# Turning the attention output of units 8 to 23 by DMA transposes instead of the PE, in a fused attention and MLP kernel

## Chip, cores, metric

One core of one Trainium2 chip. The metric is device time in microseconds (us) of one execution. One of 11 executions of the kernel before took 392 us in one series; it is not among the fast runs.

Names: PE is TensorE, which does the matmuls; ScalarE stands in profile lines as ACT, VectorE as DVE, GpSimd as POOL; SP is SyncE, which here issues the loads, the stores and the DMA transposes. PSUM is the memory that PE's products are written to.

## The reference

A linear attention with a decaying state feeds an MLP with SiLU. Cut to what matters:

```python
# r, k, v: (4 batches, 8 heads, 768 positions, 48)
for t in range(S):
    cur = einsum('bhd,bhe->bhde', u * kt, vt)
    y[:, :, t] = einsum('bhd,bhde->bhe', rt, state + cur)
    state = w[None, :, :, None] * state + einsum('bhd,bhe->bhde', kt, vt)
x = y.transpose(0, 2, 1, 3).reshape(3072, 384)
h = x @ w_in                      # 384 -> 2048
return (h * sigmoid(h)) @ w_out   # 2048 -> 384
```

## The kernel before

The sequence is cut into pieces of 128 positions. One piece of one batch is a **unit** (24 of them), and the four units of the same piece are a **chunk** `sc` (6 of them). The attention of a unit leaves `y16` with positions on the partitions. The first MLP product needs the 384 features on the partitions, so `p4` turns the tile: three PE transposes into PSUM and a ScalarE copy to `xT`.

```python
def p3e(i):
    L["y16"] = wrk.tile([128, H, D], F16, name="y16")
    nc.vector.tensor_tensor(out=L["y16"], in0=L["y"], in1=L["vu"], op=ALU.add)

def p4(i):
    ...                                    # xT: one tile for the four units of a chunk
    yT = ps.tile([128, NQ, C], F16, name="yT", tag="t", bufs=5)
    yf = L["y16"].rearrange("p h d -> p (h d)")
    for q in range(NQ):                    # NQ = 3
        nc.tensor.transpose(yT[:, q, :], yf[:, 128 * q:128 * q + 128], ident16)
    nc.scalar.copy(out=xts[sc][:, :, b, :], in_=yT)
```

The MLP of a finished chunk waits in a queue of **fillers**, which are put between the steps of the next units so that PE always has work: `l1` (three matmuls and a Silu on ScalarE; 512 columns wide, or 256 for half a chunk) and a quarter of an `l2` (four matmuls; after the fourth quarter DVE copies `osb` and SP stores it). `fill(n)` takes fillers worth n; a half-width `l1` counts one half.

```python
for i in range(B + 2, NU):                 # units 6 to 23
    ...                                    # p2: scores of unit i, then input transposes of i + 1
    fill(2)
    ...                                    # front: v cast on ScalarE, products on GpSimd for i + 1
    if i >= NIN:
        load(i + NIN)                      # r, k, v of unit i + 6: three DMAs on SP
    fill(1)
    p3y(i); p3e(i); sums(i); state(i)
    fill(2)
    p4(i)
    r16(i + 1)                             # cast of rT on ScalarE
    fill(1)
    ...
    fill(2)
    if b == B - 1:
        ...                                # l1 of the whole chunk, then its l2, join the queue
```

## Time and profile before

| | |
|---|---|
| median time | 201.92 us (201.52 to 202.05, 3 runs); 201.77 (4 runs) in the comparison with the changed kernel |
| span in the profile | 200.2 us |
| PE busy | 192.0 us, without a gap from 50 us to 197 us |
| transposes of `p4` | 72, three per unit; 0.168 us of PE per unit (units 8 to 23) |
| copies of `p4` on ScalarE | 24 x 0.478 us |
| loads, stores on SP | 72 of 192 KB, landing in 3.8 to 4.0 us; 23 of 192 KB, landing in 2.0 us |

PE's instructions overlap (three transposes of 220 ns each start within 0.17 us), so the busy length of one is not what it costs the next one. For the cost, read the time from the start of one group to the start of the next. The lines that carry this stand in the prediction.

### The profile page before, as it was taken

To read this page: it belongs to the slowest core of one execution; us is meant where nothing else is said; L and a number is where in the kernel's file an instruction comes from. 1 tells how busy PE (TensorE), PEld (TensorE's weight loads), DVE (VectorE), ACT (ScalarE), POOL (GpSimd) and SP (SyncE) were. 2 spreads that over 40 slices of the span, in tenths; PEclk is the share of its full clock that TensorE was granted. 3 is DMA by queue.
4 is the path that set the end of the run, shared out by engine and by line. 5 is a ranking of instruction groups with operands and counts; after the bars stand their busy time and mean duration, and the time that the engine had idled before them with its cause. 6 is when DMAs were issued, how large, how long until landed. Compare 5 with 4: busy or idle time off the path is not lost.

```text
span 200.2 us, 5013 instructions
## 1 busy us (share of the span) xinstructions
PE 192.0 (96%) x1973; PEld 129.8 (65%) x1973; DVE 115.1 (58%) x233; ACT 97.9 (49%) x225; POOL 115.2 (58%) x145
## 2 busy tenths in 40 slices
PE   7789999898999999999999999999999999999993
PEld 2546878786776976765666765666764666644563
DVE  6787658894757647773746864646863635510121
ACT  2655487798133652049662039662039661069300
POOL 3489969989865783768593767481748370100000
DMA  4999998999889954498521748201120001210022
GB/s 86 201 185 165 181 213 178 178 186 194 170 172 226 245 120 97 103 221 175 114 48 40 163 114 161 43 0 43 39 84 0 0 3 41 78 43 0 0 79 79
DMA packets 82207, 22.34 MB, mean 112 GB/s; under 512 B 75400, under 2 KB 82184, under 8 KB 82184
## 3 DMA queue, kind: packets, MB, share of 16 engines
q1 hardware_dynamic: 78504, 18.88, 43.7%
q0 software_dynamic: 3680, 3.15, 10.3%
q8 instruction: 15, 0.25, 0.5%
q14 instruction: 8, 0.07, 0.1%
HBM read 20.45 MB, written 4.72 MB: 126 GB/s over the span
## 4 chain that ended last, share of the span: by engine, by line
PE 84%; DVE 6%; POOL 4%; issue 3%; ACT 1%; DVEq 0%; POOLq 0%
PE ops L366 30%; PE hps L354 28%; PE ae L267 10%; PE xs L242 4%; PE y L293 3%; PE yT L342 2%; DVE am L276 2%; PE y L290 2%; POOL ku L180 1%; PE ops L380 1%; PE sps L309 1%; PE spin L125 1%; DVE pif L156 1%; POOL rku_f L186 1%; DVE y L300 1%
## 5 line engine op out<-in xcount | busy, mean ns | idle before, releaser
L357 ACT ACTIVATE gT<-hps 128x256 f16<-128x256 f32 (+1 forms) x128 | 59.5, 495 | 25.1 <-PE hps L354 23.3
L354 PE MATMUL hps<-xT,win 128*128 128x256 f16 (+1 forms) x384 | 69.9, 326 | 0.2
L366 PE MATMUL ops<-wout,gT 128*128 128x384 f16 x368 | 65.8, 326 | 0.0
L354 PEld LDWEIGHTS <-win 128*128 128x128 f16 x384 | 35.2, 98 | 22.1 <-issue 0.9
L366 PEld LDWEIGHTS <-gT 128*128 128x128 f16 x368 | 34.2, 98 | 20.9
L343 ACT COPY xT<-yT 128x384 f16<-128x384 f16 x24 | 11.5, 478 | 56.4 <-PE yT L342 56.4
L276 DVE TENSOR_TENSOR am<-ae,maskM 128x512 f16<-128x512 f32 x24 | 16.6, 691 | 32.5 <-PE ao L269 32.5
L203 POOL TENSOR_TENSOR vu<-vin,rku 128x384 f32<-128x384 f32 x23 | 19.1, 829 | 21.8 <-DVE rku L197 21.7
L370 DVE COPY osb<-ops 128x384 f32<-128x384 f32 x23 | 12.8, 556 | 32.5 <-PE ops L366 32.3
L267 PE MATMUL ae<-rk 48*128 48x128 f32 x192 | 27.7, 285 | 1.0 <-DVE rk L230 1.0
L267 PEld LDWEIGHTS ae<-rk 48*128 48x128 f32 x192 | 23.1, 187 | 8.3 <-issue 5.8
L269 PE MATMUL ao<-rk 48*128 48x128 f32 x192 | 27.7, 285 | 0.0
L253 DVE TENSOR_TENSOR rk<-xs,pif 112x512 f32<-112x512 f32 x40 | 25.6, 680 | 1.7 <-PE xs L242 1.7
L180 POOL TENSOR_TENSOR ku<-kin,u_bc 128x384 f32<-128x384 f32 x24 | 24.1, 1005 | 2.0 <-DMA kin<-in_k_dram 2.0
L186 POOL TENSOR_TENSOR rku_f<-rin,ku 128x384 f32<-128x384 f32 x24 | 24.1, 1005 | 1.9
L191 POOL TENSOR_TENSOR kc<-kin,lamC 128x384 f16<-128x384 f32 x24 | 24.0, 1002 | 0.0
L269 PEld LDWEIGHTS ao<-rk 48*128 48x128 f32 x192 | 23.1, 187 | 0.0
L323 POOL CAST stb<-st 112x384 f16<-112x384 f32 x12 | 6.0, 502 | 22.8 <-DVE st L318 22.8
L300 DVE TENSOR_TENSOR y<-y,vu 128x384 f16<-128x384 f32 x24 | 13.3, 554 | 8.7 <-PE y L293 6.5
L276 DVE TENSOR_TENSOR am<-ao,maskM 128x512 f16<-128x512 f32 x24 | 16.3, 680 | 0.0
L197 DVE TENSOR_REDUCE rku<-rku_f 128x8 f32<-128x384 f32 x24 | 13.2, 549 | 2.4 <-POOL rku_f L186 2.0
L325 POOL TENSOR_TENSOR sdec<-st,pif 112x384 f32<-112x384 f32 x16 | 13.3, 835 | 1.8 <-ACT gT L357 1.1
(74 smaller groups left out, 188.4 us busy)
## 6 DMA issues: line engine op xcount, KB each, us to landing
rin<-in_r_dram SPq DMA_DIRECT2D x24, 192.0 KB, 4.0
kin<-in_k_dram SPq DMA_DIRECT2D x24, 192.0 KB, 3.8
vin<-in_v_dram SPq DMA_DIRECT2D x24, 192.0 KB, 3.8
out_dram<-osb SPq DMA_DIRECT2D x23, 192.0 KB, 2.0
win<-in_moe_w_in_dram POOLq DMA_DIRECT2D x4, 384.0 KB, 6.0
wout<-in_moe_w_out_dram POOLq DMA_DIRECT2D x2, 768.0 KB, 10.4
out_dram<-osh SPq DMA_DIRECT2D x1, 128.0 KB, 1.7
out_dram<-osh SPq DMA_DIRECT2D x1, 64.0 KB, 1.5
```

The lines of the kernel that those rows point to most:

```text
L180: nc.gpsimd.tensor_tensor(out=L["ku"], in0=kin[i % NIN][:, :, 0:D], in1=u_bc, op=ALU.mult)
L186: nc.gpsimd.tensor_tensor(out=L["rku_f"], in0=rin[i % NIN][:, :, 0:D], in1=L["ku"], op=ALU.mult)
L191: nc.gpsimd.tensor_tensor(out=kc[i % NKC][:, :, 0:D], in0=kin[n][:, :, 0:D], in1=lamC, op=ALU.mult)
L203: nc.gpsimd.tensor_tensor(out=L["vu"], in0=vin[i % NIN], in1=L["rku"].unsqueeze(2).broadcast_to([128, H, D]), op=ALU.mult)
L253: nc.vector.tensor_tensor(out=rk[:, :, :, 64 * g:64 * g + 64], in0=xs[g][0:PR], in1=lam(g), op=ALU.mult)
L267: nc.tensor.matmul(ae[:, p, :], L["kT"][0:D, p, :], L["rT"][0:D, p, :], start=True, stop=True)
L269: nc.tensor.matmul(ao[:, p, :], L["kT"][64:PR, p, :], L["rT"][64:PR, p, :], start=True, stop=True)
L276: nc.vector.tensor_tensor(out=am, in0=a, in1=maskM.unsqueeze(1).broadcast_to([128, NP, C]), op=ALU.mult)
L300: nc.vector.tensor_tensor(out=L["y16"], in0=L["y"], in1=L["vu"], op=ALU.add)
L354: nc.tensor.matmul(hps, win[:, q, ft * 128:(ft + 1) * 128], xts[sc][:, q, b0:b1, :].rearrange("p b t -> p (b t)"), start=(q == 0), stop=(q ...
L357: nc.scalar.activation(out=gts[sc][:, ft, b0 * C:b1 * C], in_=hps, func=AF.Silu)
L366: nc.tensor.matmul(ops, gts[sc][:, ft, b * C:(b + 1) * C], wout[:, ft, :], start=(ft == 0), stop=(ft == NFT - 1))
```

## The change

The intent is to take 48 of the 72 transposes out of PE's stream and 16 copies off ScalarE. The tile now arrives by a DMA, later than before, so the fills of units 8 to 15 leave fillers over that give PE work in the meantime, and the unit's loads are issued behind the transpose.

```diff
-        L["y16"] = wrk.tile([128, H, D], F16, name="y16")
+        L["y16"] = wrk.tile([128, H, D], F16, name="y16", bufs=3)
 ...                                                   (in p4)
+        if i >= 2 * B:
+            nc.sync.dma_start_transpose(out=xts[sc][:, :, b, :],
+                                        in_=L["y16"].rearrange("p h d -> p (h d)"))
+            return
 ...                                                   (in the loop, after front)
-        if i >= NIN:
+        if NIN <= i < 2 * B:
             load(i + NIN)
 ...
         p4(i)
+        if i >= 2 * B:
+            load(i + NIN)
 ...
-        fill(2)
+        fill(1 if sc in (2, 3) else 2)
         if b == B - 1:
```

## The prediction

> **What bounds the kernel now.** A unit is one batch's 128 positions; four units make a chunk (units 8 to 11 are chunk 2), and the MLP's matmuls are queued behind the attention as fillers. I read the page first: its head (busy time by engine) and the 40 slices.
>
> ```profile
> span 200.2 us, 5013 instructions
> PE 192.0 (96%) x1973; PEld 129.8 (65%) x1973; DVE 115.1 (58%) x233; ACT 97.9 (49%) x225; POOL 115.2 (58%) x145
> ...
> PE   7789999898999999999999999999999999999993
> ...
> DMA  4999998999889954498521748201120001210022
> ```
>
> PE is the only engine near full, and its few idle tenths lie in the first quarter. A matmul's end is modelled, so a busy PE alone proves little; three more views carry it. The first is the table of stretches, which tells where PE never rests and what the others do there:
>
> ```profile
> 50.00:65.00 15.00, 15.00 (x170) 10.70 (x170) 10.46 (x20) 4.46 (x11) 10.37 (x12) 1.00 0.93 189
> 65.00:95.00 30.00, 30.00 (x337) 21.11 (x337) 18.83 (x36) 14.08 (x34) 21.18 (x26) 1.00 0.72 161
> 95.00:125.00 30.00, 30.00 (x316) 19.19 (x314) 18.83 (x36) 13.95 (x29) 19.86 (x24) 1.00 0.49 107
> 125.00:152.00 27.00, 27.00 (x297) 17.91 (x297) 17.24 (x33) 11.36 (x23) 14.79 (x18) 1.00 0.13 39
> 152.00:175.00 23.00, 23.00 (x221) 14.44 (x220) 11.21 (x20) 10.38 (x22) 8.56 (x10) 1.00 0.07 25
> ```
>
> From 50 us on PE (second figure) fills every stretch at clock 1.00; DVE, ACT and POOL have a third or more free. Second, the chain that ended last: after 48 us its long pieces are PE alone, down to the output product. Third, the list of waits: its long rows are ACT, DVE and POOL waiting for PE, while no row of PE's matmuls exceeds 1.4 us. So the time moves by what leaves PE's instruction stream after 50 us, plus any new wait put into it.
>
> What leaves is in the groups by line (after the bar: busy us, then the mean of one in ns):
>
> ```profile
> L343 ACT COPY xT<-yT 128x384 f16<-128x384 f16 x24 | 11.5, 478 | 56.4 <-PE yT L342 56.4
> ...
> L342 PE MATMUL yT<-ident,y 128*128 128x128 f16 x72 | 8.0, 220 | 0.8 <-DVE y L300 0.7
> ```
>
> and in the order of time of PE around unit 16 (start, length, both us):
>
> ```profile
> 121.52 1.46 PE L354 MATMUL hps<-xT,win 128*128 128x512 f16 x6
> 122.81 0.33 PE L342 MATMUL yT<-ident,y 128*128 128x128 f16 x3
> 122.98 2.11 PE L354 MATMUL hps<-xT,win 128*128 128x512 f16 x9
> ```
>
> The 220 ns of one transpose are latency, not cost: three start at 122.81 and the next matmul at 122.98. A unit's transposes take 0.17 us of PE. I measured that step for units 8 to 23, each from its first transpose to the next matmul: always 0.167 or 0.168 us, and the matmul before keeps its usual step.
>
> **What the Trainium skill says.** "VectorE: DVE Perf Modes", section "The three transpose paths", gives a 128x128 bf16 transpose 390 ns on TensorE and 1309 ns by the DMA crossbar. "TensorE: Matmul & The Clock Gate", section "Part 4: PE-mode transpose", says about 275 ns in one kernel, most of it access latency; the trace agrees in kind (219 ns each, but 56 ns apart). "DMA: Bandwidth & Descriptors", section "DMA Transpose (X-bar)", asks for two bytes per element, SBUF as destination and SP or ACT as issuer, which the change meets, and forbids two transposing streams at once: here all come from SP. The same page, section "Issuing engines are not separate DMA queues", says that all DMAs interleave on 16 engines, so the transposes share them with loads and stores. The trace before has no crossbar transfer; its closest, a 192 KB store of the output, lands 2.0 us after issue.
>
> **The change, part by part.**
>
> Removed from PE: 16 units x 3 = 48 transposes, 16 x 0.168 = 2.68 us, all in the saturated stretch. Their weight loads overlap other work and count no second time. Removed from ACT: 16 x 0.478 = 7.6 us, worth nothing directly, as ACT sits idle 56.4 us before just these copies. A unit now takes 6 slots of the five-deep PSUM ring instead of 7; PE shows no wait there, so again nothing.
>
> Added: 16 crossbar transfers of 128 x 384 x 2 bytes = 96 KB on SP, 1.5 MB against the 22 MB moved now. Three blocks, if the skill's 1.31 us is mostly fixed cost, make some 2 us; three in a row would be 3.9. With 0.4 us to issue, my estimate from y16 ready and SP free to landing is 2.5 to 4 us.
>
> Moved: in units 8 to 15 one filler fewer (a filler is four l2 matmuls or a full-width tile of l1; four ops matmuls take 0.65 us in the chain). PE's total work does not change: walking the fill calls in program order, the queue holds 2 leftover fillers after unit 11 and 6 after units 15, 19 and 23, where before it held none. They delay the first l1 of the new chunk, the only reader of the transposed tile. From the place where p4 stood in a chunk's last unit to that reader PE now has:
> - chunk 2: two fillers, then scores and the next input transposes (132.57 to 134.12, 1.55 us), then two fillers: 4 x 0.65 + 1.55 = 4.15 us;
> - chunk 3: eight fillers, the 1.55 and the y and state matmuls (0.55): 7.3 us;
> - chunk 4: nine fillers and the same: 7.9 us;
> - chunk 5: nine fillers alone, since no unit follows: 5.9 us.
>
> The transfer itself is ready earlier than that point or later. In the trace y16 is written about 0.7 us before p4's slot (91.37 + 0.56 against 92.73 in unit 11), but SP takes its instructions in order. In units 11 and 15 the filler just ahead of p4 ends an output tile, so SP waits for DVE's copy and issues that store first: about p4 + 1.3 us (PE's end 0.3, copy 0.56, issue 0.4). Landing is then at p4 + 3.8 to 5.3 us with my estimate: in chunk 2 that is from just in time to 1.1 us late, elsewhere hidden. I take 0.3 us of stall.
>
> The loads moved behind p4 in units 8 to 17: load(14) would go out about 71 us instead of 64.65, but its unit starts its POOL work after 100 us. They no longer stand ahead of the same unit's transpose, and the unit before's have 7 us to drain (one load lands in about 4).
>
> Sum: 201.9 - 2.7 + 0.3 = 199.5 us.
>
> **The rivals.**
>
> A. The transfer takes the place of PE's work as a wait at the chunk boundaries. For it: only 4.15 us of cover in chunk 2, a store ahead of it on SP, and a destination in three pieces per partition. Against: the three other boundaries have 6 to 8 us. At 6 us from issue to landing chunk 2 stalls about 3.1 us and the gain is gone (about 202.3); at 10 us all four stall, together some 15 to 18 us (about 215).
>
> B. SP becomes the bound: if issuing a transpose holds it for several us, stores come late, the four osb buffers run out, DVE waits and then PE. For it: SP issues one instruction at a time.
>
> ```profile
> 79.70 5.13 SPq L372 DMA_DIRECT2D out_dram<-osb  x2
> 84.93 0.39 SPq L71 DMA_DIRECT2D rin<-in_r_dram  x1
> 85.43 0.65 SPq L71 DMA_DIRECT2D kin<-in_k_dram  x1
> 86.18 0.60 SPq L71 DMA_DIRECT2D vin<-in_v_dram  x1
> ```
>
> Against: the 5.13 us there are a wait for DVE, not work; three loads and two stores use some 2.5 us of a 7.5 us unit. A transpose would have to hold SP about 4 us. That would give 202 to 206.
>
> C. The transfers collide with loads. The DMA share reads 0.93 in 50 to 65 us. But transposes begin at 70, each now ahead of its unit's loads. At most a microsecond more of landing, which only chunk 2 would feel: 200.5.
>
> D. DVE or POOL becomes the bound in units 8 to 15, now 7.55 - 0.17 - 0.65 = 6.7 us long. POOL's work is 19.9 us per four units (5.0 each), DVE's 4.7, ACT's 3.5. All fit, so PE should stay full.
>
> **Range and chances.** All of PE's saving and no stall gives 199.2; PE cannot save more than the 2.68 it spends on the removed instructions, so below 198.8 would need an effect that I don't see. Two per cent faster is 197.9: 3%. The likely spoiler is the landing time, which no row of this trace measures: up to 5 us leaves 199.2 to 200.5, 6 us about 202. Two per cent slower is above 206, which takes landings over 7.5 us or a blocked SP: 8%. Predicted 199.5 us, 8 in 10 between 198.8 and 201.6; within 2%: 89%.
>
> **What would show each step.** PE's row for L342 at x24 instead of x72, and no gap in its stretches after 50 us, confirm the saving; unit length in units 16 to 19 should fall from 7.55 to about 7.4 us. The chain should still be PE from 50 us to the end. If A holds, hps waits for the DMA of xT in PE's waits, first at chunk 2. If B holds, DVE's osb waits for a DMA of out_dram. If D holds, PE waits for am or y of DVE. The row of DMA issues gives the landing time of xT: under 4 us bears out my 0.3, over 6 refutes it. Wrong altogether I would be if PE's clock fell below 1.00 or if its steps between other matmuls changed.

## The result

The changed kernel takes 199.58 us (199.45 to 199.74, 4 runs) against 201.77 us of the kernel before (4 runs). The ratio is 0.9891, 95% interval 0.9874 to 0.9908. Ratios here are the mean time of one kernel's fast runs over the mean of the other's fast runs of the same rounds, so not quite the ratio of the medians. Predicted were 199.5 us.

The head of the page of the changed kernel, and the lines of its groups that remain of `p4` (line numbers have moved by four):

```profile
span 197.8 us, 4932 instructions
PE 189.7 (96%) x1925; PEld 127.2 (64%) x1925; DVE 115.4 (58%) x233; ACT 91.9 (46%) x209; POOL 115.1 (58%) x145
```

```profile
L347 ACT COPY xT<-yT 128x384 f16<-128x384 f16 x8 | 3.9, 482 | 7.0 <-PE yT L346 7.0
...
L346 PE MATMUL yT<-ident,y 128*128 128x128 f16 x24 | 2.7, 222 | 0.8 <-DVE y L300 0.7
```

PE has 48 matmuls fewer (with their weight loads) and ScalarE 16 copies; the counts of DVE and GpSimd are as before. What came is in the list of DMA issues (median time from issue to landing last) and in the view of the tile `xT` (how long SP is held, in ns, and the landing):

```profile
xT<-y SPq DMA_TRANSPOSE x16, 2.4
```

```profile
L340 SPq DMA_TRANSPOSE xT<-y x16: 1178/1187/1823, 63.9 to 167.3; - x16
...
DMA to landing us min/median/max: 2.3/2.4/4.5
```

One transpose holds SP for 1.19 us and the tile lands 2.4 us after the issue begins; these are medians, and of the 16 landings 13 are on record, from 2.3 to 4.5 us. The same stretches of time as before, PE busy in the second column:

```profile
65.00:95.00 30.00, 29.72 (x343) 21.04 (x341) 21.16 (x40) 12.16 (x29) 23.22 (x28) 1.00 0.70 151
95.00:125.00 30.00, 30.00 (x321) 19.23 (x320) 20.75 (x41) 13.20 (x26) 20.07 (x25) 1.00 0.56 123
125.00:152.00 27.00, 27.00 (x277) 17.15 (x276) 16.28 (x31) 10.81 (x21) 15.85 (x19) 1.00 0.28 68
```

PE is full again, but for 0.28 us between 65 and 95. The order of time shows it on PE and on ScalarE, in unit 9:

```profile
68.14 2.46 PE L358 MATMUL hps<-xT,win 128*128 128x256 f16 x21
70.88 0.49 PE L358 MATMUL hps<-xT,win 128*128 128x256 f16 x3 [0.28 <-ACT gT L361]
```

```profile
68.67 1.37 ACT L361 ACTIVATE gT<-hps 128x256 f16<-128x256 f32 x4 [0.20 <-PE hps L358]
69.94 0.61 ACT L259 CAST rT<-rk 112x512 f16<-112x512 f32 x1
70.44 1.34 ACT L361 ACTIVATE gT<-hps 128x256 f16<-128x256 f32 x4
```

PE waits there for a Silu, not for a transpose: the cast of `rT` stands between Silus. In the starts of PE's matmuls the step over this gap is 0.44 us longer than its neighbours.

Where the transfer might have hurt, at the border of chunks 1 and 2, SP and PE do this:

```profile
84.60 1.19 SPq L340 DMA_TRANSPOSE xT<-y  x1
```

```profile
86.34 1.47 PE L370 MATMUL ops<-wout,gT 128*128 128x384 f16 x8
87.65 0.81 PE L358 MATMUL hps<-xT,win 128*128 128x512 f16 x3
```

Unit 11's transpose is issued at 84.60 us and its landing is recorded at 86.89 us; the first reader runs at 87.65 us. No matmul waits for it.

### The profile page after: what moved, and what is told of

It reads as the page before. It is cut to its first block, busy times and chain, and to the rows that moved or that the text cites. A ratio compares the mean times of both kernels' runs of the same rounds, so it can differ in the third digit from the quotient of the medians.

```text
span 197.8 us, 4932 instructions
## 1 busy us (share of the span) xinstructions
PE 189.7 (96%) x1925; PEld 127.2 (64%) x1925; DVE 115.4 (58%) x233; ACT 91.9 (46%) x209; POOL 115.1 (58%) x145
## 4 chain that ended last, share of the span: by engine, by line
PE 82%; issue 5%; POOL 5%; DVE 4%; ACT 2%; POOLq 0%; DVEq 0%
PE ops L370 31%; PE hps L358 27%; PE ae L267 10%; PE xs L242 4%; PE y L293 3%; DVE am L276 2%; PE y L290 2%; POOL ku L180 2%; PE ops L384 1%; PE sps L309 1%; POOL rku_f L186 1%; PE yT L346 1%; ACT gT L361 1%; DVE y L300 1%; PE ao L269 1%
## 5 line engine op out<-in xcount | busy, mean ns | idle before, releaser
L370 PE MATMUL ops<-wout,gT 128*128 128x384 f16 x368 | 64.0, 327 | 0.0
L259 ACT CAST rT<-rk 112x512 f16<-112x512 f32 x20 | 12.3, 616 | 32.1 <-DVE rk L253 32.1
## 6 DMA issues: line engine op xcount, KB each, us to landing
wout<-in_moe_w_out_dram POOLq DMA_DIRECT2D x2, 768.0 KB, 11.3
```

What stands on the lines that cost most here:

```text
L370: nc.tensor.matmul(ops, gts[sc][:, ft, b * C:(b + 1) * C], wout[:, ft, :], start=(ft == 0), stop=(ft == NFT - 1))
```

## The experiments

Theory: the time falls by what 48 transposes cost PE, 2.68 us, less 0.44 us for the wait of unit 9; the transfer is hidden only because the short fills and the order on SP give it time. Rivals: the gain is due to ScalarE or to the new places of the fillers; the transfer is so quick that the cover is idle; the wait of unit 9 comes from the transposes' traffic.

Medians, with the kernel before of the same series at 201.75 us (1 to 4), 201.85 us (5 to 8, without the slow execution) and 201.80 us (9 and 10):

| run | time us | ratio to before, interval | PE's new wait |
|---|---|---|---|
| changed kernel | 199.58 | 0.9891 (0.9874 to 0.9908) | ScalarE 0.3 |
| 1 transposes on PE as well | 202.21 | 1.0029 (1.0016 to 1.0042) | 0.1 |
| 2 full fills | 199.98 | 0.9911 (0.9898 to 0.9923) | DMA of xT 0.9 |
| 3 before, short fills | 202.24 | 1.0024 (1.0012 to 1.0036) | ScalarE 0.5 |
| 4 cast moved | 199.27 | 0.9882 (0.9870 to 0.9895) | none |
| 5 loads ahead | 201.08 | 0.9962 (0.9949 to 0.9976) | DMA of xT 1.0, ScalarE 0.3 |
| 6 each transpose twice | 207.10 | 1.0270 (1.0242 to 1.0299) | DMA of xT 5.7, ScalarE 0.3 |
| 7 from unit 6, cast moved | 198.58, two levels | 0.9842 (0.9812 to 0.9872) | DMA of xT 1.3 |
| 8 from unit 4, cast moved | 225.08, one run | no rounds | DMA of xT 10.4, of rin 11.3, of kin 1.7 |
| 9 units 6 and 8 to 23, cast moved | 197.87 | 0.9805 (0.9791 to 0.9818) | none |
| 10 from unit 6, more cover | 198.16 | 0.9823 (0.9809 to 0.9836) | ScalarE 0.1 |

All gave correct results.

### 1. The transposes on PE as well

```diff
                                         in_=L["y16"].rearrange("p h d -> p (h d)"))
+            idle = ps.tile([128, NQ, C], F16, name="idle", tag="t", bufs=5)
+            for q in range(NQ):
+                nc.tensor.transpose(idle[:, q, :], ...)     # as in p4; nobody reads idle
             return
```

> The changed kernel, with the 48 PE transposes of units 8 to 23 put back into PE's stream, into a PSUM tile that nobody reads; the ScalarE copies stay away and the DMA still delivers the tile. If the gain is PE's instruction stream alone (my theory), this gives back 48 x 56 ns = 2.68 us: 202.2 us, at most 0.3 less where PE now gives ScalarE time in unit 9. If the gain came from the ScalarE copies or from the moved fillers and loads (rival), it stays near 199.6.

Measured 202.21 us, 2.63 us more than the changed kernel: 55 ns for each of the 48 transposes. By the starts of the units 2.51 us of it are the transposes: 15 units are 0.17 us longer, and unit 9 takes 7.23 us in both kernels, as the transposes there fall into PE's wait for ScalarE (0.11 us instead of 0.28). The other 0.1 us lies before unit 8, where the kernels do not differ. The 16 copies are still off ScalarE and the DMA still delivers the tile, so neither is where the gain came from.

### 2. Full fills

```diff
-        fill(1 if sc in (2, 3) else 2)
+        fill(2)
```

> The changed kernel with the filler count of units 8 to 15 as it was before, so no leftover fillers cover the transfer. Cover from p4's slot to the first reader falls to about 2.4, 3.0, 3.0 and 1.5 us at the four chunk boundaries, while the trace has the tile land 1.9 us (no store ahead of it) to 3.5 us (a store ahead) after that slot. My theory: PE waits for the DMA at chunks 2 and 5, 0.5 to 3 us in all, so 200.1 to 202.6 us. Rival (the short fills do nothing, the transfer is quick enough): 199.6 or a little less, as the wait of unit 9 goes too.

Measured 199.98 us, 0.40 us more. The waits of PE have a new line, and the wait for ScalarE in unit 9 is gone:

```profile
PE hps L358 <- DMA xT<-y: 0.9, 2, 0.5
```

Two waits, 0.42 us at 116.92 us (the tile of chunk 3) and 0.47 us at 173.87 us (chunk 5). At the second, unit 23's transpose lands at 174.29 us and PE goes on at 174.34. I had named chunks 2 and 5; chunk 2 passed without a wait. So the cover is needed, but it is worth only 0.9 us, and it costs the 0.44 us in unit 9; the difference of the two fits the 0.40 us of the medians.

### 3. The kernel before with short fills

```diff
-        fill(2)
+        fill(1 if sc in (2, 3) else 2)
```

> The kernel before with only the shorter fills of units 8 to 15; PE transposes and ScalarE copies stay. If fillers are only moved and ScalarE's pile-up in unit 9 comes with their new places, this is slower than before by 0.3 to 0.9 us (there is one more copy on ScalarE): 202.1 to 202.7. If the fills themselves bring part of the gain: below 201.5.

Measured 202.24 us, 0.49 us more than before. No DMA transposes are in this kernel, and yet PE waits for ScalarE in unit 9, at 70.98 us:

```profile
PE hps L354 <- ACT gT L357: 0.5, 1, 0.5
```

So the wait belongs to the new places of the fillers and not to the transposes' traffic. With one filler fewer in unit 8, more half-width `l1` tiles are left for unit 9. In the changed kernel eight of them follow the state matmuls in a row (24 matmuls, shown above), before it was six (18 matmuls) and then `l2` quarters, which need nothing of ScalarE; the cast falls into their midst.

### 4. The cast of rT moved in unit 9

```diff
-        if i + 1 < NU:
+        if i + 1 < NU and i != 9:
             r16(i + 1)
 ...
         fill(1 if sc in (2, 3) else 2)
+        if i == 9:
+            r16(i + 1)
```

> The changed kernel, with ScalarE's cast of rT for unit 10 moved behind the two fillers that follow it in unit 9. If PE's only gap after 50 us (0.28 us in the record, 0.44 us in its steps, at 70.3 us) is ScalarE doing this cast and the v cast among half-width Silus that need as long as PE's matmuls, the gap goes and the time falls 0.3 to 0.45 us: 199.2. If the gap has another cause (the transposes' traffic, PSUM), the gap stays and the time is 199.6.

Measured 199.27 us, 0.31 us less than the changed kernel; the two intervals overlap, so the record has to decide. In it unit 9 takes 6.79 us instead of 7.23, the 0.44 us of the wait. The same place, PE and then ScalarE:

```profile
68.10 2.78 PE L358 MATMUL hps<-xT,win 128*128 128x256 f16 x24
```

```profile
68.63 2.68 ACT L361 ACTIVATE gT<-hps 128x256 f16<-128x256 f32 x8 [0.19 <-PE hps L358]
71.20 0.61 ACT L259 CAST rT<-rk 112x512 f16<-112x512 f32 x1
```

All 24 matmuls run through and the cast comes after the eight Silus. A half-width `l1` takes PE three steps of 0.109 us, 0.33 us, and eight of its Silus take ScalarE 2.68 us, 0.33 us each. With no slack per tile, the 0.61 us of the cast can only be taken up by the three PSUM buffers between the two engines. Run 3 shows the wait without any DMA transpose and run 4 removes it by moving the cast, so this cause is shown.

### 5. The loads ahead of the transpose again

```diff
-        if NIN <= i < 2 * B:
+        if i >= NIN:
             load(i + NIN)
 ...
-        if i >= 2 * B:
-            load(i + NIN)
```

> The changed kernel with the loads of units 8 to 17 put back ahead of p4, so each transpose stands behind its own unit's three loads on the issuing queue. My prediction's rival C: the transpose lands 1 to 2 us later and only chunk 2, where the tile now lands 0.93 us before its reader, stalls: 199.8 to 200.7. Against it: the loads are issued some 3 us before p4's slot and land in 3.4 to 3.6 us, so they are nearly done: then 199.6 and no wait of PE for the tile, and the move was a precaution.

Measured 201.08 us, 1.5 us more than the changed kernel and past the upper end of what I expected. SP around unit 11's transpose:

```profile
82.39 0.36 SPq L376 DMA_DIRECT2D out_dram<-osb  x1
82.85 0.39 SPq L71 DMA_DIRECT2D rin<-in_r_dram  x1
83.34 0.64 SPq L71 DMA_DIRECT2D kin<-in_k_dram  x1
84.09 0.85 SPq L71 DMA_DIRECT2D vin<-in_v_dram  x1
85.03 0.77 SPq L376 DMA_DIRECT2D out_dram<-osb  x1
85.85 1.20 SPq L340 DMA_TRANSPOSE xT<-y  x1
```

I had the loads go out 3 us ahead of the transpose's slot. But a store stands before them, and SP waits 3.3 us for the copy that it stores:

```profile
SPq L376 <- DVE osb L374: 3.3, 1, 3.3
```

So they go out just ahead of the transpose. The transpose is issued 1.25 us later than in the changed kernel and takes 3.06 instead of 2.29 us to land, so it lands at 88.91 instead of 86.89 us, and PE waits 0.97 us at chunk 2 (by the starts, the step there is 1.13 us too long). Of the remaining 0.4 us I find 0.2 before unit 8 and 0.2 after the last unit's start; both are as large as the differences between profiles elsewhere. The move of the loads is therefore a working part of the change, not a precaution. The 0.77 us of longer landing comes with the loads just ahead; that their transfers make it was not tested by itself.

### 6. Each transpose twice

```diff
+            for _ in range(2):
-            nc.sync.dma_start_transpose(...)
+                nc.sync.dma_start_transpose(...)            # the same out and in_
```

> The changed kernel with every DMA transpose issued twice into the same place. If the tile's landing sets the first reader's start where my count of the cover says, the second lands 1.2 (issue alone) to 2.4 us (if it waits for the first) later: chunk 2 has 0.93 us to spare and stalls 0.3 to 1.5 us, chunks 3 to 5 have 2 us or more and do not: 199.9 to 201.1. If the issuing queue becomes the bound (rival B), stores come late, DVE's copy of the output waits, and the time rises by several us. If landing does not matter at all: 199.6.

Measured 207.10 us, 7.5 us more: far outside what I expected of the landing alone. SP's waits and PE's:

```profile
SPq L341 <- DMA xT<-y: 25.1, 16, 2.7
```

```profile
PE hps L359 <- DMA xT<-y: 5.7, 1, 5.7
```

The second transpose writes what the first wrote, so SP waits for the first to land. A pair holds SP for 3.8 to 5.0 us in units 8 to 11 (3.5 to 5.5 over all); with three loads and the stores unit 10 takes SP 8.35 us (78.28 to 86.63), while PE has a unit of 6.75 us. From unit 8's pair to unit 11's SP takes 24.2 us (63.89 to 88.08), PE three units of 20.7 us, and chunk 2 pays the lag at once. Over these units SP is the bound, but not by late stores, as I had thought: DVE's waits for output stayed as they were, and the late transposes hit first. With a single transpose, 1.2 us of SP instead of 3.8 to 5.0, there is room.

The wait costs more than its 5.7 us. Unit 12 takes 14.08 us from start to start instead of 6.74, which is 7.34 of the 7.5 us. The rest comes after the wait. The stretches of time show it; the third figure from the end of a line is the granted clock:

```profile
87.60:93.50 5.90, 0.22 (x2) 0.00 (x0) 1.35 (x3) 0.00 (x0) 1.06 (x2) 0.69 0.54 137
93.50:96.60 3.10, 3.09 (x22) 1.71 (x23) 0.88 (x3) 0.60 (x1) 0.00 (x0) 0.50 0.92 189
96.60:100.00 3.40, 3.40 (x33) 2.02 (x33) 0.85 (x2) 2.68 (x5) 2.97 (x4) 0.99 0.35 95
```

For some 3 us after the wait the clock is 0.50, and the 512-wide matmuls start 0.43 us apart instead of 0.22. Around the waits of 1.0 us in run 5 and 1.3 us in run 7 it stays at 1.00. Run 8 shows it again: 0.50 from 64.5 to 70 us, after a wait of 10.4 us.

### 7. From unit 6 on

```diff
-        if i >= 2 * B:                                  (in p4)
+        if i >= B + 2:
 ...
-        if NIN <= i < 2 * B:
-            load(i + NIN)
 ...
-        if i >= 2 * B:                                  (after p4)
+        if i >= NIN:
             load(i + NIN)
```

with the cast moved as in 4.

> The version of the late cast, with units 6 and 7 also turned by the DMA and their loads behind p4. PE loses 6 more transposes, 6 x 56 ns = 0.34 us, in a stretch where it is full from 50 us on; the first reader of their tile comes at about 64 us, and the queue ahead of them drains at about 56 us. Theory: 198.9 to 199.1. If the queue is still late with loads: PE waits for the tile of chunk 1, 199.5 or more.

Six runs gave 199.46, 199.62, 199.12, 197.90, 197.87 and 198.05 us: two levels. The profile was taken at the upper one (199.46) and shows a wait at chunk 1's first reader:

```profile
PE hps L358 <- DMA xT<-y: 1.3, 1, 1.3
```

Unit 7's transpose is issued at 61.37 us; PE waits from 62.71 to 63.99 us. The lower level is below what the removed instructions can give. The place of unit 6's `p4` tells why. Before (here from run 4, with PE transposes in unit 6):

```profile
47.47 0.34 PE L346 MATMUL yT<-ident,y 128*128 128x128 f16 x3 [0.52 <-DVE y L300]
```

PE works in order, so its transposes also waited for DVE's `y16`, 0.52 us. By the starts of the matmuls the step was 0.68 us too long there (in the kernel before, read at 47.61 us). In run 7 the matmuls go on without a stop at that place, and unit 6 takes 7.67 us instead of 8.54: 0.68 and 0.17 us for the transposes are 0.85 of the 0.87. No execution at the lower level was profiled, and why unit 7's tile comes in time in some executions and not in others is not shown.

### 8. From unit 4 on

The same with `if i >= B` in `p4`.

> The same with units 4 and 5 too. The issuing queue works in order, and before the transpose of unit 5 stand loads that wait for buffers until about 50 us in the record of before; the first reader of chunk 1's first half comes at 42 to 48 us. If the order of the queue is what limits (rival B in another place): PE waits several us for the tile, 203 to 212. If the transposes get through: 198.6.

One run, 225.08 us. PE's waits, and SP:

```profile
PE xs L242 <- DMA rin<-in_r_dram: 11.3, 1, 11.3
PE hps L358 <- DMA xT<-y: 10.4, 1, 10.4
```

```profile
60.41 0.66 SPq L71 DMA_DIRECT2D vin<-in_v_dram  x1
61.16 14.06 SPq L340 DMA_TRANSPOSE xT<-y  x2
```

The direction was foreseen, the size (203 to 212) was not. The queue's order bites twice. Unit 5's transpose stands behind loads until 61.16 us, and PE waits for it until about 64.5 us. And unit 4's transpose, issued at 34.36 us, holds up the loads behind it: `rin` of unit 6 goes out at 35.74 us instead of 28.01, lands at 46.74, and PE's input transposes wait 11.3 us for it, and 1.7 us more for `kin`. Of this I had not thought. That load took 11 us to land while the two 768 KB loads of `wout` were in flight (issued at 34.44 and 37.92 us, landed at 43.45 and 48.74). In the kernel before, loads issued in that stretch are about as slow (8.3 and 14.7 us for those issued at 34.39 and 36.38 us), but there they belong to unit 8. The lowered clock after the waits (see run 6) adds to the time.

### 9. Units 6 and 8 to 23

```diff
-        if i >= 2 * B:                                  (in p4)
+        if i == B + 2 or i >= 2 * B:
```

with the loads as in 7 and the cast as in 4.

> The version of the late cast with unit 6 turned by the DMA too, unit 7 by the PE as before. In the run from unit 6 on, three times are near 197.9 and three near 199.4, and its record (a slow one) has PE waiting 1.3 us at 62.7 us for the tile that unit 7's transpose lands too late; unit 6 became 0.87 us shorter, as PE no longer waits 0.52 us for y16 there. If that is so, here the wait cannot occur (unit 6's tile landed at 60.3) and the gain of unit 6 stays: 199.27 - 0.17 - 0.5 to 0.7 = 198.4 to 198.6, with a spread below 0.4 us. If the two levels come from elsewhere, they show here too.

Measured 197.87 us (197.62 to 197.97): one level, and lower than expected. The profile has no gap in PE after 50 us; unit 6 takes 7.67 us. PE's last matmul ends at 193.09 us against 194.06 in run 4, 0.97 us earlier: 0.87 of it is unit 6, 0.1 lies before. The median fell by 1.40 us; the other 0.4 us is after the last matmul (3.05 us to the end instead of 3.46), which I cannot assign to the edit.

### 10. From unit 6 with more cover

Run 7 with `fill(1 if sc in (1, 2, 3) else 2)`.

> The run from unit 6 on, with the shorter fill in units 6 and 7 too, so two more fillers (1.3 us) cover chunk 1's tile. Theory: the wait of 1.3 us at the first reader goes in nearly every run, all times near 197.9 (at most 198.2), unless the half-width Silus, which now come later, pile up on ScalarE at another place (up to 0.5 us).

Measured 198.16 us (197.93 to 198.41). The upper level of run 7 is gone with the wait, as in run 9; both runs fit that the wait made it. A wait for ScalarE of 0.14 us appears at 64.6 us, where the half-width Silus now fall; by the starts that unit is 0.30 us longer than in run 9 (7.09 and 6.79). It is as good as run 9 within about 0.3 us, not better.

## Why the prediction was right, step by step

- **PE bounds from 50 us on, and 48 transposes cost 2.68 us.** Right. Run 1 put them back for 2.63 us. Units 16 to 19, whose fills did not change, went from 7.56 to 7.39 us on average, as foreseen (about 7.4). Two readings on the way were loose: in the first two stretches DVE or GpSimd have 29 to 31% free and not a third, and GpSimd's long waits are for DVE, not for PE. Neither carries the sum.
- **The copies on ScalarE are worth nothing.** Right within the noise of the medians: in run 1 they stay away, and the time is 0.46 us above the kernel before, which is what the short fills alone cost in run 3 (0.49). In the records there is one exception: unit 9 takes 7.23 us in run 1 and 7.61 us in run 3, which has one copy more among its Silus. That it is the copy was not tested by itself.
- **The cover in chunk 2 is 4.15 us.** Right: in the changed kernel two fillers before 84.80 us put p4's slot at 83.50, and the reader runs at 87.65 us.
- **Landing 3.8 to 5.3 us after that slot, 0.3 us of stall.** Mis-sized: landing came 3.4 us after it, with 0.8 us to spare. I had 2.5 to 4 us from issue to landing and 2.4 were measured; within this, the issue took 1.19 us instead of the 0.4 us that I took from plain copies.
- **Rival D: everything fits, PE stays full.** Wrong in one unit. I compared averages per unit (ScalarE 3.5 us of 6.7) and did not see that in the stretch of half-width tiles ScalarE needs as long as PE. It cost 0.44 us of PE's steps (runs 3 and 4).
- **The sum.** The stall that I counted did not come, and one came that I had not counted, of about the same size. So 199.5 against 199.58 owes something to luck. From the records: 2.68 - 0.44 = 2.24 us; 0.1 lies before unit 8, and the kernel before had a hitch of 0.16 us at 64.1 us that the changed one lacks: 2.50 us, and PE's last matmul indeed ends 2.51 us earlier (197.05, 194.54). The medians differ by 2.19 us; the end after the last matmul is 0.2 us longer in the changed kernel's record.
- **Rival C, loads in the way.** No reader waited, but only because the change moves the loads. Longer landings did occur: unit 9's tile took 4.45 us and unit 10's 3.83 us, against 2.29 us for unit 11's; what made them was not tested. Where the loads went ahead (run 5) the time was 201.08 us; I had put it at 200.5, as I counted a longer landing (at most 1 us; 0.77 came) and not the order in which SP issues (1.25 us). I also placed the first transpose at 70 us; unit 8's is at 63.87 us. And the times 91.37 and 92.73 that I gave for unit 11 are unit 12's, with 92.73 taken from the chain; by the start of the first transpose (92.57) the lead is 0.64 us instead of 0.80, and unit 11's own times (85.02 and 85.66) give the same.
- **Rival B, SP as the bound.** I asked for 4 us of holding SP; run 6 gave it that and showed the bound, though by late transposes and not by late stores, and at 207.10 us instead of 202 to 206.

## What to carry to other kernels

Where PE is full, an off-loaded transpose is worth its step in PE's order (56 ns here, not the 220 ns of its bar), plus any wait that PE did in order for its input; both are read from the starts of neighbouring matmuls. Its price is the time from issue to landing (median 2.4 us, up to 4.5 here) plus whatever stands ahead of it on the issuing queue, so count the work between the old place and the first reader, and put loads that are not urgent behind it. When fillers move, check the engine that consumes them over the stretch where it is tightest, not over the mean of a unit. And do not count a long wait of PE at its length alone: after 5.7 us (run 6) another 1.5 us went into slower steps at a clock of 0.50.

## What the Trainium skill lacked or had wrong

- "DMA: Bandwidth & Descriptors", section "DMA Transpose (X-bar)": it does not say how long a small SBUF-to-SBUF transpose holds the issuing engine on this chip. Here 128x384 two-byte elements hold SP 1.18 to 1.19 us as a rule, against 0.33 to 0.52 us for the shortest plain copies.
- "VectorE: DVE Perf Modes", section "The three transpose paths", gives 1309 ns for one 128x128 block by the DMA. Three blocks in one DMA landed 2.4 us after the issue began (median of the 13 landings on record), so neither one block's time nor three times it. The page does not tell how it scales.
- "TensorE: Matmul & The Clock Gate", section "Part 4: PE-mode transpose", gives the length of one transpose (about 275 ns in a kernel; 220 ns here), not what it takes from a full PE: 56 ns by the steps, 55 ns by run 1.
